# Routing logits with the gate weights as stationary operand, turned back, and the second batch's keys ahead of its block-sum values

## The chip, the cores and the metric

The kernel runs on one core of one Trainium2 chip. The metric is the device time of one launch in microseconds (us). Before the change it is 558.69 us, the median of 3 runs (557.62 to 560.31).

## The reference, cut to what matters

Three stages follow each other: local attention with block sums, a mixture of experts with one expert for each token, and a gated feed-forward layer.

```python
k_sum = k.reshape(B, H, nb, block, D).max(axis=3)
v_sum = v.reshape(B, H, nb, block, D).mean(axis=3)
...
x = attn_out.transpose(0, 2, 1, 3).reshape(B * S, H * D)     # 1536 tokens x 512
logits = x @ w_gate                                          # 8 experts
e_idx = np.argmax(logits, axis=1)
...
eom = 1.0 / (1.0 + np.exp(-(x @ w_output_gate)))
for e in range(E):
    mask = e_idx == e
    h = np.maximum(x[mask] @ w1[e], 0.0)
    out[mask] = gate_w[mask, None] * eom[mask, e, None] * (h @ w2[e])
...
gate = 1.0 / (1.0 + np.exp(-(x @ w_gate)))
return (gate * (x @ w_val)) @ w_out
```

B is 2 batches, S 768 positions, H 8 heads, D 64; a block has 32 positions and the local window 16.

## The kernel before

The order of all instructions is written out by hand; each engine works through its own queue in that order, and a semaphore wait at the head of a queue holds all that stands behind it.

**Attention** goes over 12 tiles of 128 queries (`T` from 0 to 11, six for each batch, `TB` = 6). The steps of a tile are functions. `spread_q` brings a tile's queries into the form that the score products take (on ScalarE, for two tiles on VectorE). `s1` computes masked scores in two halves, each into one PSUM bank of the ring "A" (3 banks); VectorE takes their minimum (`nm`), ScalarE the exponential (`a`). `s3` transposes `a` into the ring "B" (2 banks), and ScalarE copies it (`aT`). `s4` multiplies by the values into the one bank pair "C", and VectorE normalises (`rs`, then the tile's rows in `w2r` or `late`). `s6` transposes the result (`xT`, copied by VectorE in the first batch and by ScalarE in the second). `s7` multiplies it by `wgo`, the 16 columns of both gate weights, into a bank of "A", and VectorE copies the logits to `lg`. In loop step T the program issues `s3(T)`, `s1(T + 2)`, `s4(T)`, and `s6` and `s7` of an earlier tile.

Four parts prepare a batch: `load_k` and `ksum` (key maxima of the blocks, on VectorE, written into the key tile `kg`), `load_vr` and `vsum_part` (block sums of the values, on GpSimd or VectorE), `load_v`, and `place_sums`, which turns the sums on TensorE (line 286) and puts them into the value tiles. SyncE issues all these transfers in program order.

**Routing** of a batch is the generator `route`: one-hot choices, ranks by TensorE (lines 415 to 420), and scatters of the rows. `pick_two` and `find_first` choose the first two experts; `find_first` compares positions in six VectorE instructions (`place`, line 143). `make_table` writes the list of work items.

**Experts** are work items `i` of up to 256 tokens. `split1` and `split2` split an expert's weights into a high half (ScalarE, line 131) and a low half (VectorE, line 134); `item_T` transposes the tokens and splits them (`xTh`, `xTl`); `item_A(f)` is the first layer for 128 hidden columns, into a bank of "A" that VectorE releases with `hl` (line 655); `item_B(f)` is the second layer. Matmuls on split operands take three passes. The feed-forward layer behind it (lines 1136 and 1177) fills more than half of the time.

Of the kernel before, what the change touches and what calls it, by code (L numbers as in the profile page):

```python
# [10 lines left out]
F32 = mybir.dt.float32  # L11
# [18 lines left out]
TB = 6  # L30
NT = B * TB
# [77 lines left out]
def moe_kernel(tc, A, out):  # L109
# [153 lines left out]
    def vsum_part(b, c):  # L263

        if b not in vsum:
            vsum[b] = at.tile([128, 4, 32], F32, tag="vs", bufs=1, name=f"vs{b}")
        if b == 0 and c > 1:
            red(vsum[b][:, c, 0:NB], vrt[b, c], ALU.add)
        else:
            t, n = vrt[b, c], BLK // 2  # L270
            while n > 1:
                G.tensor_tensor(out=t[:, :, 0:n], in0=t[:, :, 0:n], in1=t[:, :, n:2 * n], op=ALU.add)
                n //= 2
            G.tensor_tensor(out=vsum[b][:, c, 0:NB], in0=t[:, :, 0], in1=t[:, :, 1], op=ALU.add)
# [100 lines left out]
    def s7(T):  # L375
        xT = st.pop(("xT", T))
        lt = bank("A", 3)
        for c in range(4):
            PE.matmul(lt[:, 0:16], xT[:, c], wgo[:, c], start=c == 0, stop=c == 3)
        V.tensor_copy(lg[:, T], lt[:, 0:16])  # L380


# [441 lines left out]
    with tc.manual_schedule():  # L824
# [19 lines left out]
            ksum(0, p)  # L844

        w2h = w2l = hh = hl = None
        q6, q8 = [], []
        order = {0: (), 1: (0,), 2: (1,), 3: (2,), 4: (3, 4)}
        ahead = {0: ((1,), ()), 1: ((2,), ()), 2: ((3,), ()), 3: ((4,), (5,))}
        spread_q(0)  # L850
# [5 lines left out]
        for T in range(NT):  # L856
            now = order.get(T, (T,))
            first, then = ahead.get(T, ((T + 2,), ()) if T < NT - 2 else ((), ()))
            q7, late7 = [t for t in q6 if t < TB or T == NT - 1], [t for t in q6 if t >= TB and T < NT - 1]
            if T < 2:  # L860
                for half in range(2):
                    s1(T + 1, (half,))
                    if T == 1 and half == 0:
                        place_sums(0)
                    s3(T, (half,))
                    if T == 0:
                        vsum_part(0, 2 + half)
                if T == 1:
                    spread_q(3)
                    spread_q(4)  # L870
            else:
                if T < NT - 1:
                    s3(T)
                if T == NT - 2:
                    s3(T + 1)
                for t in q8:
                    s7(t)
                for t in now[:-1]:
                    s4(t)
                for t in first:  # L880
                    s1(t, (0,))
                for t in q6:
                    s6(t)
                if T < NT - 3:
                    spread_q(T + 3)
                for t in first:
                    s1(t, (1,))
                if T == 7:
                    run(g, 1)
                    p1, ff = pick_two(), find_first()  # L890
                    run(p1, 1)
                    item_regs(0)
                if T == 8:
                    run(ff, 9)
                if T > 8:
                    run(g, 1)
                if T == 11:
                    item_T(0, 0, ("A", 3))
                    item_T(0, 1, ("A", 3))
            for t in now[-1:]:  # L900
                s4(t)
            for t in then:
                s1(t)
            for t in q7:
                s7(t)
            q6, q8 = list(now), late7

            if T == 0:
                load_q(4)
                for c in range(4):  # L910
                    load_vr(1, c)
            if T == 1:
                load_q(5)
                load_k(1, (0, 1))
                load_q(6)
                load_k(1, (2, 3))
                load_q(7)
                load_v(1, 0)
                load_v(1, 1)
                SP.dma_start(out=ck, in_=A["ck"])  # L920
                SP.dma_start(out=ckb, in_=A["ckb"])
                G.iota(gix, pattern=[[128, 2]], base=0, channel_multiplier=1)
                G.tensor_copy(slot, gix)
                for t0, t1 in ((0, 6), (6, 12)):
                    G.memset(xr[t0, t1][:, :, DM + 2:XW], 0.0)
                    G.iota(xr[t0, t1][:, :, DM + 1].bitcast(I32), pattern=[[128, t1 - t0]], base=128 * t0, channel_multiplier=1)
                G.memset(gidx, OOB)
                for c in range(4):
                    vsum_part(1, c)
            if T == 2:  # L930
                ksum(1, 0)
                ksum(1, 1)
            if T == 3:
                ksum(1, 2)
                ksum(1, 3)
            if 2 < T < 7:
                load_q(T + 5)
            if T == 4:
                place_sums(1)
                V.memset(low, 0.0)  # L940
                for e in range(1, 8):
                    V.memset(low[:, e, 0:e], 1.0)
            if T == 5:
                G.memset(xg[0], 0.0)
                first_st.close()
                mB_ = pool(moeA2_st, "mA2", "left")
                w1h = mB_.tile([128, 4, F], F32R, name="w1h")
                w1l = mB_.tile([128, 4, F], F32R, name="w1l")
                xTh = mB_.tile([128, 4, SLOT], F32R, name="xTh")
                xTl = mB_.tile([128, 4, SLOT], F32R, name="xTl")  # L950
                store_x(0, 3)
            if T == 6:
                store_x(3, 6)
                g = route(0)
                run(g, 2)
            if T == 7:
                run(ff, 1)
                load_w(reg["e", 0], None, range(4))
            if T > 7:
                run(g, 1)  # L960
            if T == 9:
                G.memset(xg[1], 0.0)
                split1(0)
            if T == 10:
                split1(1)
                split1(2)
            if T == 11:
                run(g, 9)
                load_w(reg["e", 0], None, range(4, 8))
                split1(3)  # L970
# [8 lines left out]
        hl = mB.tile([128, 8, SLOT], F32R, name="hl")  # L979
        run(p1, 1)  # L980
        item_A(0)
        s6(11)
        item_A(1)
        run(p1, 1)
# [2 lines left out]
        item_A(2)  # L987
        s7(11)
        item_A(3)
        run(p1, 1)  # L990
        item_regs(1)
        load_w(reg["e", 1], reg["e", 1] != reg["e", 0], range(4))
# [6 lines left out]
        item_A(6)  # L999
        split2(1)  # L1000
        item_A(7)
        run(g, 1)
        tb = make_table()
        split2(2)
        split2(3)
# [5 lines left out]
        for i in range(NSTAT):  # L1011
# [6 lines left out]
            if i:  # L1018
                for f in range(8):
                    item_A(f)  # L1020
                    if f % 2 == 0:
                        split2(f // 2)
                    elif i > 1:
                        run(bg, 1)
                    if i == 1:
                        if f in (1, 3, 4, 5):
                            run(tb, 1)
                        if f == 5:
                            item_regs(2)
                            item_gather(2, gidx[:, 2])  # L1030
            if i < NSTAT - 1:
# [2 lines left out]
            for f in range(8):  # L1034
                item_B(f, yp)
                if f % 2 == 0 and i < NSTAT - 1:
                    split1(f // 2)
                if f in (4, 5) and (f == 4 or i < NSTAT - 2):
                    item_T(i + 1, f - 4)
                if i and f in ((1, 2, 3) if i == 1 else (1, 2, 3, 6)):  # L1040
                    run(bg, 1)
                if not i and f == 0:
                    run(g, 9)
                    tail_st.close()

                    ws_st = ExitStack()
                    wsp_ = pool(ws_st, "wsp", "right")
                    yr_st = ExitStack()
                    yrp = pool(yr_st, "yrp", "right")
                    yrt = [yrp.tile([128, XW], F32, name=f"yr{k}") for k in range(4)]  # L1050
                    for t in yrt:
                        G.memset(t, 0.0)
                    cv_st = ExitStack()
                    cv = pool(cv_st, "cv", "right")

                    todo = [("w", f, k) for f in range(2) for k in range(2)]
                    bg = background(todo)
                    for k in todo[:3]:
                        load_raw(k)
                if not i and f in (1, 3, 7):  # L1060
                    run(tb, 1)
                if i == 5 and f in (0, 2, 3, 6):
                    t = (0, 2, 3, 6).index(f)
                    y_T(t)
                    load_y(t + 4, few)
                if i == 5 and f == 7:
                    split2(0)
# [180 lines left out]
```

## Time and profile before

| | |
|---|---|
| median of 3 runs | 558.69 us |
| profiled execution | 559.4 us, span 557.4 us |
| TensorE busy | 536.9 us, 96% of the span |
| VectorE busy | 385.8 us, 69% |
| ScalarE busy | 214.1 us, 38% |
| GpSimd busy | 126.7 us, 23% |
| mean granted clock of TensorE | 0.993 |

A busy TensorE means that some matmul is in flight; matmuls overlap, so the sum of durations is longer than the time they take. In the profile PE is TensorE, PEld its weight loads, DVE VectorE, ACT ScalarE, POOL GpSimd and SP SyncE. The attention stage lies before 91 us, the work items reach to about 250 us, and the feed-forward layer follows.

### The profile page before, as it was taken

To read this page: it belongs to the slowest core of one execution; us is meant where nothing else is said; L and a number is where in the kernel's file an instruction comes from. 1 tells how busy PE (TensorE), PEld (TensorE's weight loads), DVE (VectorE), ACT (ScalarE), POOL (GpSimd) and SP (SyncE) were. 2 spreads that over 40 slices of the span, in tenths; PEclk is the share of its full clock that TensorE was granted. 3 is DMA by queue.
4 is the path that set the end of the run, shared out by engine and by line. 5 is a ranking of instruction groups with operands and counts; after the bars stand their busy time and mean duration, and the time that the engine had idled before them with its cause. 6 is when DMAs were issued, how large, how long until landed. Compare 5 with 4: busy or idle time off the path is not lost.

```text
span 557.4 us, 8974 instructions
## 1 busy us (share of the span) xinstructions
PE 536.9 (96%) x3236; PEld 457.5 (82%) x3236; DVE 385.8 (69%) x735; ACT 214.1 (38%) x391; POOL 126.7 (23%) x151
## 2 busy tenths in 40 slices
PE   7799989989999999999999999999999999999995
PEld 4688979888989989867888888888888888888884
DVE  5677677789778687853687899999998763323320
ACT  3766775645546555643212112121112351212110
POOL 2673144182102100000001111111111062112211
PEclk9989999999999999998999999999999999999999
DMA  8991465972478403216123233233232000001010
GB/s 313 414 409 64 152 232 179 378 278 75 137 269 255 171 32 108 77 59 197 49 76 96 94 114 99 89 114 113 80 110 76 1 1 38 20 38 39 19 39 38
DMA packets 31983, 71.62 MB, mean 128 GB/s; under 512 B 3056, under 2 KB 11712, under 8 KB 31936
## 3 DMA queue, kind: packets, MB, share of 16 engines
q1 hardware_dynamic: 28816, 60.96, 31.5%
q0 software_dynamic: 3120, 10.06, 5.3%
q8 instruction: 26, 0.43, 0.3%
q14 instruction: 21, 0.17, 0.1%
HBM read 72.53 MB, written 11.33 MB: 150 GB/s over the span
## 4 chain that ended last, share of the span: by engine, by line
PE 34%; issue 14%; POOL 5%; ACT 0%; POOLq 0%; DVE 0%; DVEq 0%; ACTq 0%
PE ps_A L1136 18%; PE ps_B L1136 15%; POOL out_dram L1180 3%; POOL yb L134 2%; PE ps_B L746 1%; POOLq L1244 0%; ACT yb L131 0%; ACT gs L131 0%; DVE yt L141 0%; DVE gg L137 0%; POOLq L1180 0%; POOL yt L706 0%; POOLq L1084 0%; DVEq L137 0%; POOLq L134 0%
## 5 line engine op out<-in xcount | busy, mean ns | idle before, releaser
L1136 PE MATMUL ps_A<-yb,wh 128*128 128x512 f32 x312 | 97.7, 394 | 2.0 <-DVE yt L141 2.0
L1177 PE MATMUL ps_A<-yb,gs 128*128 128x512 f32 x432 | 98.1, 389 | 0.0
L1177 PEld LDWEIGHTS ps_A<-yb,gs 128*128 128x128 f32 x432 | 81.1, 188 | 16.8
L1136 PE MATMUL ps_B<-yb,wh 128*128 128x512 f32 x264 | 81.3, 389 | 0.0
L1136 PEld LDWEIGHTS ps_A<-yb,wh 128*128 128x128 f32 x312 | 58.4, 190 | 13.9 <-issue 2.4
L1136 PE MATMUL ps_A<-yb,wl 128*128 128x512 f32 x156 | 61.0, 391 | 0.0
L134 POOL TENSOR_TENSOR wl<-cvw,wh 128x512 fp32r<-128x512 f32 x20 | 26.7, 1334 | 137.9 <-ACT wh L131 137.9
L1136 PEld LDWEIGHTS ps_B<-yb,wh 128*128 128x128 f32 x264 | 49.6, 188 | 10.2
L1145 ACT ACTIVATE sg<-ps_A 128x512 f32<-128x512 f32 x36 | 21.5, 596 | 91.3 <-PE ps_A L1136 91.3
L652 PE MATMUL ps_A<-xTl,w1h 128*128 128x256 f32 x192 | 54.4, 284 | 1.5 <-DVE xTl L134 1.5
L652 PE MATMUL ps_A<-xTh,w1h 128*128 128x256 f32 x192 | 54.6, 284 | 0.0
L652 PE MATMUL ps_A<-xTh,w1l 128*128 128x256 f32 x192 | 54.3, 283 | 0.0
L1136 PE MATMUL ps_B<-yb,wl 128*128 128x512 f32 x132 | 51.3, 389 | 0.0
L131 ACT ACTIVATE gs<-gg 128x768 fp32r<-128x768 f32 x24 | 20.3, 847 | 69.5 <-PE ps_A L1177 67.4
L134 DVE TENSOR_TENSOR gs<-gg,gs 128x768 fp32r<-128x768 f32 x24 | 23.0, 958 | 34.2 <-ACT gs L131 34.1
L143 DVE TENSOR_SCALAR cva<-cva 128x512 f32<-128x512 f32 x72 | 43.3, 602 | 1.9
L134 DVE TENSOR_TENSOR w2l<-w2r,w2h 128x1024 fp32r<-128x1024 f32 x28 | 34.2, 1225 | 10.2 <-ACT w2h L131 10.0
L661 PE MATMUL yp<-w2h,hh 128*128 128x512 f32 x96 | 39.0, 406 | 0.0
L652 PEld LDWEIGHTS ps_A<-xTl,w1h 128*128 128x128 f32 x192 | 36.8, 192 | 1.9 <-DVE xTl L134 1.8
L661 PE MATMUL yp<-w2h,hl 128*128 128x512 f32 x96 | 37.5, 391 | 0.0
L661 PE MATMUL yp<-w2l,hh 128*128 128x512 f32 x96 | 37.5, 391 | 0.0
L134 DVE TENSOR_TENSOR w1l<-w1r,w1h 128x1024 fp32r<-128x1024 f32 x28 | 34.1, 1221 | 4.2 <-ACT w1h L131 4.1
(229 smaller groups left out, 967.0 us busy)
## 6 DMA issues: line engine op xcount, KB each, us to landing
w1r<-in_w_dram SPq DMA_DIRECT2D x28, 512.0 KB
w2r<-in_w_dram SPq DMA_DIRECT2D x28, 512.0 KB
raw<-in_wgv_dram SPq DMA_DIRECT2D x24, 512.0 KB
vt<-in_vv_dram SPq DMA_DIRECT2D x12, 520.0 KB
raw<-in_wo_dram SPq DMA_DIRECT2D x12, 512.0 KB
kg<-in_kg_dram SPq DMA_DIRECT2D x8, 496.0 KB
y_c<-yt SPq DMA_DIRECT2D x13, 256.5 KB
yr<-y_c SPq DMA_DIRECT2D x12, 256.5 KB
```

The source lines that it names most:

```text
L131: SC.activation(out=o, in_=i, func=AF.Copy)
L134: (eng or V).tensor_tensor(out=o, in0=i, in1=h.bitcast(F32), op=ALU.subtract)
L143: V.tensor_scalar(out=o, in0=a, scalar1=s1, scalar2=s2, op0=op0, op1=op1)
L652: PE.matmul(hp, w[:, c, s], x[:, c], start=n == 0, stop=n == 11)
L661: PE.matmul(yp[h], x[:, f, s], w[:, f], start=f == 0 and n == 0, stop=f == 7 and n == 2)
L746: PE.transpose(tp[:, c], r[:, c * 128:c * 128 + 128], ident)
L1136: PE.matmul(pp, w[:, c], x[:, c], start=n == 0, stop=n == 11)
L1145: SC.activation(out=sg, in_=pp, func=AF.Sigmoid)
L1177: PE.matmul(po, g2[:, x, f % 6], yb[f // 4][w][:, f % 4], start=f == 0 and n == 0, stop=f == 11 and n == 2)
L1180: d = G.indirect_dma_start(out=out[:, :], out_offset=bass.IndirectOffsetOnAxis(ap=row_id[:, t:t + 1].bitcast(U32), axis=0), in_=ot, in_off ...
```

## The change

`s7` now takes the gate weights as stationary operand and the tokens as moving one, so its product has 16 rows and 128 columns. VectorE copies it to a tile `lT`, and a new step `s8` transposes it back on TensorE; VectorE then copies the result to `lg` as before. Both steps take a bank of "A". `s8` of a tile stands later in the order than its `s7`: behind the next `s3` in the first batch, behind `s6` of the next tile in the second. For tile 5, `s7` stands ahead of `s4(6)`.

Besides: the keys of the second batch are loaded ahead of its block-sum values, query tiles 4 and 5 are spread later, the key maxima of the second batch are all taken in step 3, and the last of its four block sums goes to VectorE. The first split of the first expert's weights moves behind `s3` of the last two tiles. One step of the second batch's routing moves behind the first `item_B`, the token transposes of item 1 move two steps ahead, and the fills of the row buffers `yrt` move to item 1.

```diff
-        if b == 0 and c > 1:
+        if c > 1 + b:
             red(vsum[b][:, c, 0:NB], vrt[b, c], ALU.add)
...
         for c in range(4):
-            PE.matmul(lt[:, 0:16], xT[:, c], wgo[:, c], start=c == 0, stop=c == 3)
+            PE.matmul(lt[0:16, 0:128], wgo[:, c], xT[:, c], start=c == 0, stop=c == 3)
+        st["lT", T] = tl_.tile([16, 128], F32, tag="lT", bufs=2, name=f"lT{T}")
+        V.tensor_copy(st["lT", T], lt[0:16, 0:128])
+
+    def s8(T):
+        lt = bank("A", 3)
+        PE.transpose(lt[:, 0:16], st.pop(("lT", T)), ident[0:16, 0:16])
         V.tensor_copy(lg[:, T], lt[:, 0:16])
...
                 if T == 1:
                     spread_q(3)
-                    spread_q(4)
             else:
                 if T < NT - 1:
                     s3(T)
+                if T == 3:
+                    spread_q(5)
                 if T == NT - 2:
                     s3(T + 1)
+                    split1(0)
+                for t in q9:
+                    s8(t)
                 for t in q8:
                     s7(t)
...
                 for t in q6:
                     s6(t)
-                if T < NT - 3:
+                for t in q8:
+                    s8(t)
+                if 2 < T < NT - 3:
                     spread_q(T + 3)
                 for t in first:
                     s1(t, (1,))
+                if T == 2:
+                    spread_q(4)
+                if T == 3:
+                    ksum(1, 0)
+                    ksum(1, 1)
...
+            if T == TB:
+                s7(TB - 1)
             for t in now[-1:]:
                 s4(t)
             for t in then:
                 s1(t)
+            if T == TB:
+                s8(TB - 1)
+                q7 = []
             for t in q7:
                 s7(t)
-            q6, q8 = list(now), late7
+            q6, q8, q9 = list(now), late7, q7
 
             if T == 0:
                 load_q(4)
+                load_q(5)
+                load_k(1, range(4))
+            if T == 1:
+                load_q(6)
                 for c in range(4):
                     load_vr(1, c)
-            if T == 1:
-                load_q(5)
-                load_k(1, (0, 1))
-                load_q(6)
-                load_k(1, (2, 3))
                 load_q(7)
...
-                for c in range(4):
+                for c in range(3):
                     vsum_part(1, c)
-            if T == 2:
-                ksum(1, 0)
-                ksum(1, 1)
             if T == 3:
                 ksum(1, 2)
                 ksum(1, 3)
+                vsum_part(1, 3)
...
                 G.memset(xg[1], 0.0)
-                split1(0)
...
         item_A(0)
+        s8(10)
         s6(11)
...
         s7(11)
         item_A(3)
+        s8(11)
...
         item_A(7)
-        run(g, 1)
         tb = make_table()
...
                         if f == 5:
+                            for t in yrt:
+                                G.memset(t, 0.0)
                             item_regs(2)
...
-                if f in (4, 5) and (f == 4 or i < NSTAT - 2):
-                    item_T(i + 1, f - 4)
+                f0 = 4 if i else 2
+                if f in (f0, f0 + 1) and (f == f0 or i < NSTAT - 2):
+                    item_T(i + 1, f - f0)
...
-                    for t in yrt:
-                        G.memset(t, 0.0)
```

**VectorE, loop steps 2 and 3.** `nm` are the minima of scores, `ks` and `kt` the key maxima, `rs` the normalisation; names end in running numbers. Before, between the first group of key maxima and the second:

```order
L255 COPY kg_107<-ks_490 128x6x24
L146 TENSOR_REDUCE nm_517<-ps_A 128x4
L372 COPY xT_528<-ps_B 128x512
L146 TENSOR_REDUCE nm_538<-ps_A 128x4
L141 TENSOR_SCALAR rs_561<-xp_544 128x8
L360 RECIPROCAL rs_561<-rs_561 128x8
L137 TENSOR_TENSOR w2r<-xp_544,rs_561 128x512
L146 TENSOR_REDUCE nm_573<-ps_A 128x4
L146 TENSOR_REDUCE nm_584<-ps_A 128x4
L380 COPY lg<-ps_A 128x16
L146 TENSOR_REDUCE ks_596<-kg_107 128x6x2
```

After, the same stretch:

```order
L146 TENSOR_REDUCE nm_502<-ps_A 128x4
L372 COPY xT_513<-ps_B 128x512
L146 TENSOR_REDUCE nm_523<-ps_A 128x4
L146 TENSOR_REDUCE ks_529<-kg_107 128x6x2
...
L255 COPY kg_107<-ks_536 128x6x24
L141 TENSOR_SCALAR rs_560<-xp_543 128x8
L360 RECIPROCAL rs_560<-rs_560 128x8
L137 TENSOR_TENSOR w2r<-xp_543,rs_560 128x512
L146 TENSOR_REDUCE nm_572<-ps_A 128x4
L146 TENSOR_REDUCE nm_583<-ps_A 128x4
L381 COPY lT_594<-ps_A 16x128
L146 TENSOR_REDUCE ks_596<-kg_107 128x6x2
```

Both groups of key maxima now stand behind the minima of tile 4, with the normalisation of tile 2 and the minima of tile 5 between them; a copy `lT` is new.

**VectorE and TensorE, loop step 8.** `late` is the normalised tile 7, `place` the comparisons of `find_first`. VectorE before:

```order
L137 TENSOR_TENSOR late<-xp_1008,rs_1025 128x512
L143 TENSOR_SCALAR place<-ckb,o_f_983,r_pf_979 128x256 x6
L380 COPY lg<-ps_A 128x16
L146 TENSOR_REDUCE nm_1066<-ps_A 128x4
L146 TENSOR_REDUCE nm_1087<-ps_A 128x4
```

VectorE after:

```order
L137 TENSOR_TENSOR late<-xp_1028,rs_1045 128x512
L143 TENSOR_SCALAR place<-ckb,o_f_1003,r_pf_999 128x256 x6
L381 COPY lT_1078<-ps_A 16x128
L146 TENSOR_REDUCE nm_1087<-ps_A 128x4
L386 COPY lg<-ps_A 128x16
L146 TENSOR_REDUCE nm_1111<-ps_A 128x4
L146 TENSOR_REDUCE place<-ps_M 128x2
```

TensorE after, with the gate product of tile 6 (`xT`, `wgo`), the scores of tile 10 in two halves, the transposes of tile 7 (`late`) and the turn of tile 6 (`lT`):

```order
L344 MATMUL ps_B<-ident,a_857 128x128 x8
L379 MATMUL ps_A<-xT_971,wgo 16x128 x4
L312 LDWEIGHTS cmb
L312 MATMUL ps_A<-cmb 128x512
L316 MATMUL ps_A<-kg_107,qz_113 128x128 x4
L370 MATMUL ps_B<-ident,late 128x128 x4
L385 MATMUL ps_A<-ident,lT_1078 128x16
L312 LDWEIGHTS cmb
L312 MATMUL ps_A<-cmb 128x512
L316 MATMUL ps_A<-kg_107,qz_113 128x128 x4
```

The copy of tile 6's logits keeps its place behind `place`, but is now what the turn on TensorE waits for, and the second half of the scores stands behind the turn.

**VectorE and TensorE, loop steps 10 and 11.** `w1l` are low halves of weights, `late` the normalised tiles 9 and 10. VectorE before:

```order
L137 TENSOR_TENSOR late<-xp_1202,rs_1219 128x512
L134 TENSOR_TENSOR w1l<-w1r,w1h 128x4x256
L380 COPY lg<-ps_A 128x16
L141 TENSOR_SCALAR rs_1288<-xp_1271 128x8
L360 RECIPROCAL rs_1288<-rs_1288 128x8
L137 TENSOR_TENSOR late<-xp_1271,rs_1288 128x512
L134 TENSOR_TENSOR w1l<-w1r,w1h 128x4x256 x2
L380 COPY lg<-ps_A 128x16
```

VectorE after:

```order
L137 TENSOR_TENSOR late<-xp_1230,rs_1247 128x512
L134 TENSOR_TENSOR w1l<-w1r,w1h 128x4x256
L381 COPY lT_1288<-ps_A 16x128
L386 COPY lg<-ps_A 128x16
L141 TENSOR_SCALAR rs_1320<-xp_1303 128x8
L360 RECIPROCAL rs_1320<-rs_1320 128x8
L137 TENSOR_TENSOR late<-xp_1303,rs_1320 128x512
L134 TENSOR_TENSOR w1l<-w1r,w1h 128x4x256 x2
L381 COPY lT_1336<-ps_A 16x128
L386 COPY lg<-ps_A 128x16
```

TensorE after, from the score transposes of tiles 10 and 11 on:

```order
L344 MATMUL ps_B<-ident,a_1080 128x128 x8
L344 MATMUL ps_B<-ident,a_1192 128x128 x8
L379 MATMUL ps_A<-xT_1210,wgo 16x128 x4
L370 MATMUL ps_B<-ident,late 128x128 x4
L385 MATMUL ps_A<-ident,lT_1288 128x16
L354 MATMUL xp_1303<-vt_111,aT_1255 64x65 x16
L379 MATMUL ps_A<-xT_1295,wgo 16x128 x4
L370 MATMUL ps_B<-ident,late 128x128 x4
L385 MATMUL ps_A<-ident,lT_1336 128x16
L647 MATMUL ps_A<-ident,xg_87 128x128 x8
```

The copies `lT` of tiles 8 and 9 stand where the copies to `lg` stood, behind one and behind two weight splits; on TensorE the value products of tile 10 and the token transposes stand behind the two turns.

## Rows read from the trace of the kernel before

**Rows 1.** The page, part 1: busy us (share of the span) x instructions.

```profile
PE 536.9 (96%) x3236; PEld 457.5 (82%) x3236; DVE 385.8 (69%) x735; ACT 214.1 (38%) x391; POOL 126.7 (23%) x151
```

**Rows 2.** Waits of TensorE over the span: total us, times, longest us.

```profile
PE ps_B L370 <- ACT aT L345: 2.6, 2, 2.4
...
PE ps_A L1136 <- DVE yt L141: 2.0, 1, 2.0
...
PE ps_B L344 <- ACT aT L345: 1.7, 2, 1.3
...
PE ps_A L652 <- DVE xTl L134: 1.5, 1, 1.5
...
PE ps_M L415 <- DVE cum L146: 0.6, 1, 0.6
```

**Rows 3.** Timeline, 20 to 37 us: start, duration, engine; in brackets idle before.

```profile
25.61 1.28 ACT L239 ACTIVATE qz<-xg 64x512 f32<-64x512 f32 x2 [2.28 <-DMA xg<-in_q_dram]
...
28.89 1.91 PE L316 MATMUL ps_A<-kg,qz 128*128 128x128 f32 x8
...
35.41 1.05 PE L316 MATMUL ps_A<-kg,qz 128*128 128x128 f32 x8
```

**Rows 4.** Windows: busy PE, PEld, DVE, ACT, POOL, then clock, DMA share, GB/s.

```profile
29.00:30.00 1.00, 1.00 (x7) 1.00 (x6) 0.40 (x1) 0.16 (x1) 0.92 (x2) 0.50 1.03 417
...
118.00:119.00 1.00, 0.27 (x2) 0.27 (x3) 1.00 (x3) 0.52 (x1) 0.70 (x2) 1.00 1.03 419
...
253.00:254.00 1.00, 1.00 (x6) 0.90 (x5) 0.00 (x0) 0.24 (x1) 0.00 (x0) 0.50 0.07 16
```

**Rows 5.** Timeline of TensorE, 48 to 58 us.

```profile
48.74 1.06 PE L286 MATMUL sp<-ident,vs 128*24 128x128 f32 x16 [0.33 <-DVE lg L380]
...
55.08 1.96 PE L379 MATMUL ps_A<-wgo,xT 128*128 128x16 f32 x16
...
56.88 1.07 PE L344 MATMUL ps_B<-ident,a 128*128 128x128 f32 x8
```

**Rows 6.** Groups by form, TensorE, 0 to 130 us: busy us, mean ns.

```profile
L286 PE MATMUL sp<-ident,vs 128*24 128x128 f32 x32 | 2.3, 275 | 1.2 <-POOL vs L274 0.9 <-DVE lg L380 0.3
```

**Rows 7.** Timeline of VectorE, 15 to 45 us.

```profile
15.41 0.95 DVE L146 TENSOR_REDUCE vs<-w1r 128x24 f32<-128x768 f32 x1
...
41.50 0.54 DVE L146 TENSOR_REDUCE ks<-kg 128x12 f32<-128x384 f32 x1
...
44.15 0.16 DVE L141 TENSOR_SCALAR rs<-xp 128x8 f32<-128x8 f32 x1
...
45.19 0.68 DVE L146 TENSOR_REDUCE nm<-ps_A 128x4 f32<-128x512 f32 x1
```

**Rows 8.** Timeline of VectorE and TensorE, 70 to 73 us.

```profile
70.89 1.62 DVE L143 TENSOR_SCALAR place<-ckb,o_f,r_pf 128x256 bf16<-128x256 bf16 x6
...
72.43 0.17 DVE L380 COPY lg<-ps_A 128x16 f32<-128x16 f32 x1
...
71.59 0.38 PE L312 MATMUL ps_A<-cmb 67*128 67x512 bf16 x1
```

**Rows 9.** Timeline of ScalarE and TensorE, 81 to 88 us.

```profile
81.31 1.07 ACT L131 ACTIVATE w1h<-w1r 128x1024 fp32r<-128x1024 f32 x1
...
82.25 1.09 ACT L345 COPY aT<-ps_B 128x512 f32<-128x512 f32 x2
...
85.26 1.15 PE L354 MATMUL xp<-vt,aT 128*64 128x65 f32 x32
...
87.74 0.63 PE L370 MATMUL ps_B<-ident,late 128*128 128x128 f32 x4 [0.33 <-DVE late L137]
```

**Rows 10.** Timeline of VectorE, 82 to 121 us.

```profile
82.41 1.23 DVE L134 TENSOR_TENSOR w1l<-w1r,w1h 128x1024 fp32r<-128x1024 f32 x1 [0.69 <-ACT w1h L131]
...
87.51 2.35 DVE L134 TENSOR_TENSOR w1l<-w1r,w1h 128x1024 fp32r<-128x1024 f32 x2
...
120.96 0.42 DVE L655 SCALAR_TENSOR_TENSOR hl<-ps_A,hh 128x256 fp32r<-128x256 f32 x1
```

More of the change, by code (lines that the diff above doesn't have):

```diff
@@ L846, in moe_kernel @@
         w2h = w2l = hh = hl = None
-        q6, q8 = [], []
+        q6, q8, q9 = [], [], []
         order = {0: (), 1: (0,), 2: (1,), 3: (2,), 4: (3, 4)}
```

## Prediction

> **What bounds the kernel now.** I read the page first: TensorE is busy for 96% of the span [rows 1], so time can be won only where TensorE waits or where its own instructions get cheaper. The waits of TensorE are few and nearly all lie before 120 us [rows 2]: 2.4 us in one piece on the ScalarE copies of the probabilities, 1.3 us on the same kind of copy later, 1.5 us on VectorE's low half of the first expert's tokens, 0.6 us on the counts of routing, and 2.0 us in a place the change doesn't touch. Behind the 2.4 us stands a transfer: ScalarE sat 2.28 us in front of the query copy of tile 4 until its data landed, and the copies that TensorE wanted were queued behind it [rows 3]. [...] From 120 us on there is nearly no wait, so what the front gains or loses reaches the end.
>
> **Gate matmuls.** Before, a tile's logits are eight TensorE instructions that move 16 columns under 128 columns of weights; two tiles take 56.88 - 55.08 = 1.80 us, so 0.90 each [rows 5]. After, eight instructions move 128 columns under 16 columns of weights. The trace has two neighbours. Transposes of 128x128 move as many columns and go at 1.07 us for eight, about 0.11 each when pipelined [rows 5]. The block-sum transposes move 128 columns under 24 of weights: sixteen in 1.06 us, about 0.06 each [rows 5]. But one of these lasts 275 ns [rows 6], more than four starts, and they write alternately to partitions 32 and 96: two run side by side. The gate products all write partitions 0 to 15, so I take the transposes: 0.9 us, no gain; bounds 0.5 and 0.9. The turn back is two instructions more with 128 columns of weights, a quarter of the old eight: 0.22 us. Two of the twelve lie inside the next part; ten are 2.2 us.
>
> [...]
>
> **The start of the second batch's work (tiles 2 to 5).** Query copies 4 and 5 move on ScalarE behind the exponentials that TensorE needs; the 2.4 us wait goes, and with it the slow clock, at least 1.91 - 1.05 = 0.86 us. On SyncE's queue, the keys of batch 1 come ahead of its block-sum values; TensorE is then served later with values, which have until the block-sum transposes at 48.74 [rows 5]; I cost that at nothing, with GpSimd's idle time as cover (one of four sums moves to VectorE). TensorE would be 3.3 us ahead. What is late next is VectorE: the key maxima of batch 1, two groups of about 44.15 - 41.50 = 2.65 us [rows 7], now both lie after the minima of tile 4, and behind them a block sum of 0.95 [rows 7]. Ahead of tile 3's normalisation stand: a minimum 0.7 [rows 7], a group 2.65, a normalisation 1.1 (from 86.4 to 87.51 [rows 9, 10]), two minima 1.3, a group 2.65, the sum 0.95, two small copies 0.35: 9.7 us. From the end of tile 4's scores, 36.46 before and about 33.2 after [rows 3], that gives 42.9 for tile 3's normalisation in place of 44.15 [rows 7]: 1.25 of the 3.3. The durations overlap by some tenths, and a 0.33 us wait at 48.74 goes too [rows 5]. I take -2.0, bounds -3.3 and -1.2.
>
> **The copies of the turned logits.** Each turn back waits for a copy on VectorE, and VectorE works in order. Before, the copy of the logits held nobody on TensorE; now the next scores, value products or expert matmuls are queued behind the turn. At three places a long piece stands ahead of the copy.
> (a) Tile 6: six placements, 1.62 us, end only at 72.43, where the logits copy starts (0.17) [rows 8]. TensorE wants to go on at 71.59 [rows 8]. With the handing over, 72.74 - 71.59 = +1.15. A small wait of TensorE on ScalarE just behind it is swallowed (0.2, what the longest of the two on those copies leaves [rows 2]): +0.95.
> (b) Tile 8: the first weight split has moved behind the copies of both last tiles. That takes away the 1.3 us wait, of which about 0.3 stays: -1.0. But VectorE's half of the split stands ahead of tile 8's copy. From the end of the last score transposes: a ScalarE copy 0.55 (two take 1.09), the high half 1.07, the low half 1.23, the logits copy 0.2 [rows 9, 10]: 3.05. TensorE comes after gate products 0.9 and transposes 0.45: 1.35. Wait +1.7.
> (c) Tile 9: two splits, 2.35 us, end at 89.86; with copy and handing over 90.17 [rows 10]. TensorE has finished its transposes at about 87.74 + 0.45 = 88.2 [rows 9]. Wait +1.95, in the order as it stands, since both count from the value products at 85.26.
>
> **The first expert.** The rank matmuls go behind six matmuls of the second layer: the 0.6 us wait is covered by their 1.4 us; -0.6. The token transposes of item 1 move two steps ahead; VectorE's low halves then come ahead of two weight splits: -1.5. What is late next is the same VectorE queue: without gaps up to the first hidden half at 120.96 [rows 10], and nothing is taken from it. The fourth hidden tile needs the PSUM bank which that half releases. All of that queue starts later by what the front lost, so the wait passes to this bank nearly whole: +1.4, bounds 0 (it fits) and 1.5 (the whole of the old wait). The fills of the row buffers move to an idle stretch of GpSimd; nothing.
>
> **Sum.** +2.2 - 2.0 + 0.95 - 1.0 + 1.7 + 1.95 - 0.6 - 1.5 + 1.4 = +3.1 us. It is made on the profiled execution, which took 559.4 (span 557.4), 0.7 above the median of 558.69; I put it on the median: 561.8.
>
> **Rivals.**
> 1. The clock falls in (c). A wait of 2.0 us was followed by 0.50, one of 1.5 not [rows 4]; (c) is 1.95, with 1.7 shortly before. Price 0.86 for one group of scores and as much again for its neighbours, about 1.6: 563.4. Against it: the predicted wait is on the edge.
> 2. The gate products do run at the pace of the block-sum transposes, 0.5 us. It counts in the six tiles where TensorE isn't held by VectorE: 6 x 0.4 = 2.4: 559.4. For it: a row with few weight columns exists; against it: that row has two column groups.
> [...]
> 3. Faster: the copies don't hold TensorE, because VectorE is through with the splits and placements when TensorE comes. (a), (b), (c) lose 0.95 + 1.7 + 1.95 = 4.6; the sum is -1.5, and if the bank wait is also absent -2.9: 557.2 to 555.8. It decides where each copy is done within about 1.3 us of the transposes before it. The order of VectorE's queue speaks against it.
> 4. The change doesn't win the second batch's start, because VectorE's key maxima take all of it or because the query data land later: -2.0 becomes 0: 563.8.
>
> **How the numbers follow.** Forecast 0.50 (560.3 to 563), rival 1 0.15, rival 2 0.15, rival 3 0.12, rival 4 0.08. A measurement here can tell about 0.5%, 2.8 us, from no change: the bounds are 555.9 and 561.5. Slower: half of the forecast and a little more, 0.27, with rivals 1 and 4: 0.50. Faster: most of rival 3 with what is left over of rival 2 when both meet: 0.12. Same: 0.38. The range leaves out about 1 in 10 on each side: 557.2, the upper end of rival 3, to 563.6, between rivals 1 and 4.
>
> **What would show it.** In the trace after, TensorE's long waits should be on the copy of the turned logits, three of them, 1.2 to 2 us, around 71, 85 and 90 us; no wait of 2 us on ScalarE at 25 us and a clock of 1.00 from 24 to 36; the gate products at about 0.11 us from start to start. The first expert's first matmul should start about 3 us later than before, and no wait on the low token half near 117. Wrong I am if the gate products go at 0.06, if the copies come early, or if the expert starts earlier than before.

## The result and the profile after

The changed kernel took 563.69 us (median of 11 runs, 562.38 to 565.78); the kernel before took 559.38 us beside it (11 runs). The ratio is 1.0085, with a 95% interval of 1.0067 to 1.0103: about 4.75 us more. The forecast was 3.1 us more, 561.8. The profiled execution of the changed kernel took 563.34 us, with a span of 561.4 us.

The page's part 1 and the waits of TensorE over the span (total us, times, longest us):

```profile
PE 541.0 (96%) x3248; PEld 456.6 (81%) x3248; DVE 389.8 (69%) x748; ACT 213.7 (38%) x391; POOL 124.2 (22%) x146
```

```profile
PE ps_A L385 <- DVE lT L381: 4.9, 4, 1.7
...
PE ps_A L1156 <- DVE yt L141: 2.2, 1, 2.2
PE ps_A L658 <- DVE hl L661: 1.0, 2, 0.7
...
PE ps_B L370 <- ACT aT L345: 0.6, 1, 0.6
```

TensorE is busy for 4.1 us more [rows 1]. The 2.4 us wait on the copied probabilities and the 1.5 us wait on the low token half are gone, and the 1.3 us one has shrunk to 0.4 [rows 2]. In their place stands one new line of 4.9 us: the turn back (L385) waits for the copy of the turned logits, lT. TensorE's timeline has the three long waits and a shorter one, and VectorE's has what stands ahead of each of the long ones:

```profile
38.81 0.23 PE L385 MATMUL ps_A<-ident,lT 16*128 16x16 f32 x1 [0.62 <-DVE lT L381]
...
46.58 1.06 PE L286 MATMUL sp<-ident,vs 128*24 128x128 f32 x16 [0.68 <-DVE w2r L137]
...
63.93 0.66 PE L370 MATMUL ps_B<-ident,late 128*128 128x128 f32 x4 [0.60 <-ACT aT L345]
...
67.91 1.05 PE L379 MATMUL ps_A<-xT,wgo 128*16 128x128 f32 x8
68.89 0.39 PE L312 MATMUL ps_A<-cmb 67*128 67x512 bf16 x1
...
72.09 0.23 PE L385 MATMUL ps_A<-ident,lT 16*128 16x16 f32 x1 [1.00 <-DVE lT L381]
72.25 0.39 PE L312 MATMUL ps_A<-cmb 67*128 67x512 bf16 x1
...
82.42 1.14 PE L344 MATMUL ps_B<-ident,a 128*128 128x128 f32 x8 [0.40 <-ACT aT L345]
...
86.65 0.23 PE L385 MATMUL ps_A<-ident,lT 16*128 16x16 f32 x1 [1.52 <-DVE lT L381]
...
91.65 0.23 PE L385 MATMUL ps_A<-ident,lT 16*128 16x16 f32 x1 [1.74 <-DVE lT L381]
91.81 1.09 PE L647 MATMUL ps_A<-ident,xg 128*128 128x128 f32 x8
92.83 1.91 PE L354 MATMUL xp<-vt,aT 128*64 128x65 f32 x32
```

```profile
70.22 1.62 DVE L143 TENSOR_SCALAR place<-ckb,o_f,r_pf 128x256 bf16<-128x256 bf16 x6
71.76 0.27 DVE L381 COPY lT<-ps_A 16x128 f32<-16x128 f32 x1
...
85.18 1.23 DVE L134 TENSOR_TENSOR w1l<-w1r,w1h 128x1024 fp32r<-128x1024 f32 x1 [3.00 <-ACT w1h L131]
86.32 0.27 DVE L381 COPY lT<-ps_A 16x128 f32<-16x128 f32 x1
...
89.06 2.35 DVE L134 TENSOR_TENSOR w1l<-w1r,w1h 128x1024 fp32r<-128x1024 f32 x2
91.33 0.27 DVE L381 COPY lT<-ps_A 16x128 f32<-16x128 f32 x1
```

What to see: at 72, 87 and 92 us TensorE waits 1.00, 1.52 and 1.74 us, and each time the 16x128 copy of 0.27 us comes right behind six placements or one or two halves of a weight split. The copy is short; its place in VectorE's queue is what costs. The fourth wait, 0.62 us at 38.81, was not forecast; it is 1.54, 1.15 and 1.60 us in experiments 2, 3 and 8. No run shows what it costs by itself: experiment 9, with the old gate products, waits 0.71, 0.58 and 0.84 us in the same stretch for other things. Eight gate products take 68.89 - 67.91 = 0.98 us from their start to the next instruction, and a turn back 72.25 - 72.09 = 0.16. Behind the third wait the 32 value products last 1.91 us instead of the usual 1.15 [rows 9]; the window there shows why (busy PE, PEld, DVE, ACT, POOL, then clock, DMA share, GB/s):

```profile
94.00:95.00 1.00, 1.00 (x16) 0.81 (x15) 0.60 (x3) 0.54 (x1) 0.00 (x0) 0.50 0.92 324
```

The granted clock is 0.50. From 92 to 97 us the five windows show 0.99, 0.50, 0.50, 0.50 and 0.80, which loses 0.01 + 3 x 0.50 + 0.20 = 1.7 us. The block-sum transposes start at 46.58 instead of 48.74 [rows 5], the first expert's first matmul at 96.47 instead of 91.17: 5.3 us later, 1.7 of them the slow clock of this one execution, where about 3 were forecast. The new wait of 0.60 us at 63.93 is one that the prediction didn't have.

### The profile page after: what moved, and what is told of

Read it like the earlier page. It is cut to its first block, busy times and chain, and to the rows that moved or that the text cites. A ratio compares the mean times of both kernels' runs of the same rounds, so it can differ in the third digit from the quotient of the medians.

```text
span 561.4 us, 9007 instructions
## 1 busy us (share of the span) xinstructions
PE 541.0 (96%) x3248; PEld 456.6 (81%) x3248; DVE 389.8 (69%) x748; ACT 213.7 (38%) x391; POOL 124.2 (22%) x146
## 4 chain that ended last, share of the span: by engine, by line
PE 34%; issue 14%; POOL 5%; ACT 0%; POOLq 0%; DVE 0%; DVEq 0%; ACTq 0%
PE ps_A L1156 18%; PE ps_B L1156 15%; POOL out_dram L1200 3%; POOL yb L134 1%; PE ps_B L752 1%; POOLq L1264 0%; ACT yb L131 0%; ACT gs L131 0%; DVE yt L141 0%; DVE gg L137 0%; POOLq L1200 0%; POOL yt L712 0%; POOLq L1104 0%; DVEq L137 0%; POOLq L134 0%
## 5 line engine op out<-in xcount | busy, mean ns | idle before, releaser
L658 PEld LDWEIGHTS ps_A<-xTh,w1h 128*128 128x128 f32 x192 | 36.8, 191 | 2.2 <-DVE hl L661 1.4
```

Of the source, the lines that this page charges most:

```text
L658: PE.matmul(hp, w[:, c, s], x[:, c], start=n == 0, stop=n == 11)
```

## The experiments

Each was timed in five rounds beside the kernel before. The last two columns are worked out: the mean of the granted clocks that the timed runs list, and the time against before at one common clock. For that, a straight line was laid through the 199 runs of these kernels and of before on three chips, with a level for each kernel and each chip and one slope; the slope is 0.36 us per 0.001 of mean clock.

| kernel | us, median | ratio to before, 95% | mean clock | us against before at one clock |
|---|---|---|---|---|
| before (83 runs) | 558.58 to 559.95 | 1 | 0.9932 | 0 |
| changed | 563.69 | 1.0085 (1.0067 to 1.0103) | 0.9954 | not in the line: no second kernel on its chip |
| 1 old gate products | 556.79 | 0.9965 (0.9948 to 0.9982) | 0.9957 | -1.70 |
| 2 wait filled | 563.74 | 1.0089 (1.0062 to 1.0116) | 0.9953 | +5.17 |
| 3 turns later | 561.55 | 1.0044 (1.0019 to 1.0069) | 0.9960 | +3.30 |
| 4 front undone | 563.25 | 1.0110 (1.0073 to 1.0146) | 0.9955 | +5.92 |
| 5 front alone | 558.38 | 0.9976 (0.9952 to 1.0000) | 0.9948 | -0.90 |
| 6 first expert alone | 560.43 | 1.0007 (0.9985 to 1.0028) | 0.9921 | -0.35 |
| 7 split alone | 559.52 | 0.9983 (0.9960 to 1.0006) | 0.9928 | -0.90 |
| 8 turns later, other bank | 560.58 | 1.0008 (0.9986 to 1.0030) | 0.9950 | +0.95 |
| 9 all but the logits | 555.56 | 0.9947 (0.9926 to 0.9969) | 0.9947 | -2.50 |
| 10 front and split | 556.11 | 0.9954 (0.9936 to 0.9973) | 0.9962 | -1.54 |
| 11 front, split, rank | 556.24 | 0.9959 (0.9942 to 0.9976) | 0.9960 | -1.59 |

**1. Old gate products, the rest of the change kept.** In the changed kernel:

```
-            PE.matmul(lt[0:16, 0:128], wgo[:, c], xT[:, c], ...)
-        st["lT", T] = tl_.tile([16, 128], F32, ...)
-        V.tensor_copy(st["lT", T], lt[0:16, 0:128])
+            PE.matmul(lt[:, 0:16], xT[:, c], wgo[:, c], ...)
+        V.tensor_copy(lg[:, T], lt[:, 0:16])
     def s8(T):
+        pass
```

> The changed kernel with the gate products of before (128 columns of weights, 16 columns moved, logits copied at once) and no turn back; all other edits of the change stay. Theory: the turned logits cost 4.3 us in three waits on the copy (1.00, 1.52, 1.74), 1.7 us in the slower clock behind the third, 10 x 0.16 = 1.6 us in turns and 10 x 0.05 = 0.5 us in dearer gate products, together 8.1; some wait on the probabilities comes back at the end. Time 555.6 us, 554.5 to 557.5, which is below before. Rival: the other edits win nothing that lasts (the start of the second batch and the first expert give back what they gain), then the time is that of before, 558.5 to 560.

Measured: 556.79 us, below before and about 6.7 us below the changed kernel (1.0085 - 0.9965 = 0.0120). The rival falls: the other edits win, and the logits lose more than they win. The 8.1 us of the theory held the 1.7 us of the slow clock; without it the sum is 6.4. Tile 5's gate products still stood ahead of its value products in this kernel, with the same late wait:

```profile
64.05 0.66 PE L370 MATMUL ps_B<-ident,late 128*128 128x128 f32 x4 [0.55 <-ACT aT L345]
...
65.65 0.17 PE L418 MATMUL ps_M<-cum,ckb 128*128 128x16 bf16 x1
```

**2. The third wait filled with useless work.** Ahead of tile 9's turn back: `for k in range(12): PE.transpose(w[:, 0:128], ident, ident)`, into a bank that nobody reads.

> The changed kernel with twelve extra 128x128 transposes, some 1.4 us of useless TensorE work whose result nobody reads, put into the 1.74 us wait ahead of tile 9's turn back. Theory: the clock fell behind this wait because TensorE stood idle; filled, the granted clock stays at 1.00 between 92 and 97 us and the kernel with more work is faster by 1.7 us: 562.0, 561.2 to 562.8. Rival: the clock falls there for another reason, or the fall costs nothing: 563.7, 563.2 to 565.

Measured: 563.74 us, no gain; the ratio is 1.0089, against 1.0085 for the changed kernel. In its trace the wait shrinks to 0.43 us, the transposes cost nothing and the clock stays at 1.00:

```profile
90.85 1.47 PE L897 MATMUL ps_M<-ident 128*128 128x128 f32 x12
92.75 0.23 PE L385 MATMUL ps_A<-ident,lT 16*128 16x16 f32 x1 [0.43 <-DVE lT L381]
```

But the fourth experiment keeps the whole wait of 1.74 us, and its clock doesn't fall either (timeline, and the window that answers to the one above):

```profile
92.88 0.23 PE L385 MATMUL ps_A<-ident,lT 16*128 16x16 f32 x1 [1.74 <-DVE lT L381]
...
94.06 1.16 PE L354 MATMUL xp<-vt,aT 128*64 128x65 f32 x32
```

```profile
94.00:95.00 1.00, 1.00 (x34) 0.94 (x32) 0.64 (x2) 1.00 (x3) 0.00 (x0) 1.00 0.80 137
```

So the fall behind this wait belongs to the profiled execution of the changed kernel and not to each run. That idleness causes it isn't refuted by this. That filling the wait pays 1.7 us (0.0030) in the median is just outside the noise: the ratio rose by 0.0004, give or take 0.0032.

**3 and 8. Each turn back one step later; then also another bank.** Experiment 3 moves `s8(t)` of tiles 6 to 10 behind the gate products of the next tile, tile 9's and 10's behind hidden tiles of the first expert. Experiment 8 adds:

```
-                    item_T(0, 1, ("A", 3))
+                    item_T(0, 1)
```

> The changed kernel with each turn back of tiles 6 to 10 issued one step later on TensorE, behind the gate products of the next tile (tile 9's behind the first hidden tile of the first expert); nothing is left out. Theory: VectorE has made the copies by then, the three waits (4.3 us) and the slow clock (1.7 us) go: 557.7 us, 556.7 to 559. Rival: the waits only pass on, to the token transposes or the first expert's matmuls, whose weight and token halves come from the same VectorE queue: 561.5 to 563.5.

> The kernel with the turns back one step later, and beside it the second token transposes of the first item write the other pair of PSUM banks. Theory: in the kernel with the turns later these transposes waited 1.30 us for the bank that tile 9's copy on VectorE frees; with a bank that this copy doesn't hold the wait goes: 560.3 us, 559.6 to 561. Rival: the same VectorE queue holds the next user of a bank or the first expert's token halves: 561.2 to 562.

Experiment 3 won 1.0085 - 1.0044 = 0.0041, 2.3 us; its 561.55 us lie at the lower end of the rival's range. The first two waits are gone; the third passed on, not through the turn but through its PSUM bank. The second token transposes take the bank which tile 9's copy has yet to read:

```profile
88.90 0.60 PE L647 MATMUL ps_A<-ident,xg 128*128 128x128 f32 x4
90.80 0.66 PE L647 MATMUL ps_A<-ident,xg 128*128 128x128 f32 x4 [1.30 <-DVE lT L381]
```

With the other pair of banks (experiment 8) nothing waits there, and the 560.58 us lie in the theory's range:

```profile
88.50 0.60 PE L647 MATMUL ps_A<-ident,xg 128*128 128x128 f32 x4
88.94 0.60 PE L647 MATMUL ps_B<-ident,xg 128*128 128x128 f32 x4
```

From the changed kernel to this one the ratio falls by 1.0085 - 1.0008 = 0.0077, 4.3 us (1.6 to either side is noise); the three waits together are 1.00 + 1.52 + 1.74 = 4.26. In the traces less of it lasts. From the block sums to the wait on the output rows it is 256.95 - 47.70 = 209.25 us in experiment 2, whose third wait is filled but lasts as long, and 253.20 - 47.23 = 205.97 here: 3.3 us less, with a new wait of 0.51 us on the way. So the close match of 4.3 and 4.26 is partly luck.

```profile
47.70 1.06 PE L286 MATMUL sp<-ident,vs 128*24 128x128 f32 x16 [0.68 <-DVE w2r L137]
...
256.95 0.73 PE L1160 MATMUL ps_A<-yb,wh 128*128 128x512 f32 x2 [2.15 <-DVE yt L141]
```

```profile
47.23 1.06 PE L286 MATMUL sp<-ident,vs 128*24 128x128 f32 x16 [0.68 <-DVE w2r L137]
...
77.28 0.38 PE L312 MATMUL ps_A<-cmb 67*128 67x512 bf16 x1 [0.51 <-DVE lg L386]
...
253.20 0.73 PE L1157 MATMUL ps_A<-yb,wh 128*128 128x512 f32 x2 [2.21 <-DVE yt L141]
```

The kernel is level with the one before: the turned logits have eaten all that the other edits win, even without the three waits.

**4 and 5. The front undone, the front alone.** The loads, query copies, key maxima and block sums at the start of the second batch go back to their old places in the changed kernel (4), or to the new ones in the kernel before (5), as in the diff.

> The changed kernel with the start of the second batch's work (query, key and value loads, query copies 4 and 5, key maxima, block sums) as before. Theory: this part won 2.2 us at the block-sum transposes, and its loss reaches the end: 565.9 us, 565 to 567, with the 2.4 us wait and the clock of 0.50 near 28 us back. Rival: its gain is taken back by the later waits on VectorE, which stay where they are: 563 to 564.2.

> The kernel before with only the start of the second batch's work changed (queries, keys and values loaded in the new order, query copies 4 and 5 later, key maxima 0 and 1 of the second batch after tile 4's scores, one block sum on VectorE). Theory: from the value products at 21 us to the block-sum transposes it saves 1.6 us (26.2 to 25.3 us in three kernels that have it against 27.1 to 27.5 in two that don't), and this reaches the end: 557.1 us against 558.7, 556.3 to 557.8. Rival: what it saves is spent before the end, at the copies of the probabilities around 64 and 83 us, where ScalarE is no earlier than before: 558.2 to 559.2.

Undone, the median of 563.25 us lies in the rival's range, but two of the six runs took 566.20 and 567.55 us, at a mean clock of 0.992 and 0.989, and the ratio rose by 1.0110 - 1.0085 = 0.0025, 1.4 us, no more than noise (0.75 us against experiment 2 at one clock). Alone, the front wins 0.0024, 1.3 us, with an interval from 0 to 2.7. All of these are less than the 2.2 us which the profile seemed to show, though the noise doesn't exclude it. What the front saves hangs on the clock: the long wait on the probabilities stood in four of the profiles, and only in two of these did the clock fall behind it, to 0.50. In experiment 4 it was 2.43 us long, the clock stayed at 1.00, and from the first value products at 20.74 us to the block sums it took 27.1 us; before, with the fall, 48.74 - 21.26 = 27.5; with the front alone 47.19 - 22.11 = 25.1. The other one of the four without a fall, experiment 6, has 46.87 - 21.01 = 25.9, so that there the front would have saved 0.8 by this kernel, and next to nothing by experiments 1, 9, 10 and 11, which have the front and the old gate products and take 25.5 to 25.8.

**7. The first split alone.** `split1(0)` behind tile 11's copies instead of at the end of tile 9's step.

> The kernel before with only the first weight split moved behind the copies of the last tiles' probabilities. Theory: the 1.3 us wait shrinks to 0.4 and 0.4 comes back at the next transposes: -0.5, 558.2 us, 557.4 to 558.9. Rival: the split's low half comes so late that the next normalisation, or the first expert, waits for all of it: 559 to 560.

0.0017, 0.95 us, with an interval that holds nothing to 2.2. Its trace has what was expected: 0.39 us in place of 1.3 at the copies, and 0.74 at the next transposes. Further on the rank matmuls wait 2.18 us instead of 0.62.

```profile
82.30 1.15 PE L344 MATMUL ps_B<-ident,a 128*128 128x128 f32 x8 [0.39 <-ACT aT L345]
...
87.55 0.63 PE L370 MATMUL ps_B<-ident,late 128*128 128x128 f32 x4 [0.74 <-DVE late L137]
```

**6, 10 and 11. The first expert's edits alone; front and split; these and the rank matmuls.** The edit of 11 against 10 is one line, a `run(g, 1)` less behind the first expert's last hidden tile.

> The kernel before with only the first expert's edits (rank matmuls behind six matmuls of the second layer, token transposes of item 1 two steps ahead, the fills of the row buffers later). Theory: the waits of 0.6 and 1.5 us go and 1.0 us on the PSUM banks of hidden tiles come: -1.1, 557.6 us, 556.8 to 558.2. Rival: the banks take all that is won, since VectorE's queue sets the pace there: 558.3 to 559.2.

> The kernel before with the front and the first weight split alone. If the parts add up: 0.9976 x 0.9983 = 0.9959 (0.994 to 0.998). Against the kernel that has the first expert's edits too it says what these are worth: theory, nothing, since the 2.1 us of waits that they take away come back at the PSUM banks (2.6 us on the low hidden halves in the profile of these edits alone); rival, they win about 1.1 us when the front is early, and this kernel is slower than that one by 0.002.

> The kernel with the front and the split, and beside them only the rank matmuls behind six matmuls of the second layer. Theory: the wait on the counts, 0.6 us before, 1.2 with the front alone and 2.2 with the split alone, is the one edit of the first expert that lasts: 0.6 to 1.5 us below the kernel without it, ratio 0.994 to 0.995. Rival: the low hidden halves hold the PSUM banks anyhow: no difference.

Alone the edits give no gain that can be measured. Experiment 10 shows that front and split add up: 0.9954 measured, 0.9959 expected. With 11 the rival holds, but by another wait: the rank matmuls' 0.62 us is passed whole to the low token half, which waited 1.45 us in experiment 10 and 2.16 in 11:

```profile
102.86 0.17 PE L415 MATMUL ps_M<-cum,ckb 128*128 128x16 bf16 x1 [0.62 <-DVE cum L146]
...
116.71 0.39 PE L652 MATMUL ps_A<-xTl,w1h 128*128 128x256 f32 x1 [1.45 <-DVE xTl L134]
```

```profile
115.94 0.39 PE L652 MATMUL ps_A<-xTl,w1h 128*128 128x256 f32 x1 [2.16 <-DVE xTl L134]
```

The edit of the rank matmuls alone pays nothing. That it pays together with the token transposes is argued from experiment 9; the token transposes were not moved by themselves. With both and the front early (experiment 9) the first expert loses 1.0 us on the banks, and alone (experiment 6) 2.6:

```profile
PE ps_A L652 <- DVE hl L655: 2.6, 3, 1.2
```

From the first expert's first matmul to the third item's it is 50.1 us in experiment 9 and 50.9 in 10: 0.8 us. In the median the difference is 0.55 us and no more than noise.

**9. Everything but the logits.** The kernel before with front, split and first expert's edits; against experiment 1 tile 5's gate products stand where they stood before.

> The kernel before with the front, the first weight split and the first expert's edits, and nothing of the logits part; against the kernel with the old gate products it differs only in tile 5, whose gate products stand behind its successors' scores again, as before, and not ahead of the value products. Theory: the other place of tile 5's gate products delays tile 5's successors by 0.6 to 0.8 us (a 0.55 us wait on the probabilities at 64 us, 18.2 us from the block sums to the rank products in place of 17.45), so this kernel is below the one with the old gate products: ratio to before 0.995 (0.9935 to 0.9965). Rival: that delay is swallowed by the wait on the splits at 82 us or by the first expert, and the ratio stays at 0.9965.

555.56 us, the fastest of all and below both kernels. Against experiment 1 it is 0.0018, 1.0 us, lower, in the theory's range, but the intervals overlap. In the traces the difference is plain: from the block sums to the rank products 64.02 - 46.56 = 17.46 us here, as before, and 65.65 - 47.44 = 18.21 in experiment 1, with no wait on the probabilities here:

```profile
46.56 1.06 PE L286 MATMUL sp<-ident,vs 128*24 128x128 f32 x16 [0.66 <-DVE lg L380]
64.02 0.17 PE L415 MATMUL ps_M<-cum,ckb 128*128 128x16 bf16 x1
...
248.15 0.73 PE L1139 MATMUL ps_A<-yb,wh 128*128 128x512 f32 x2 [1.99 <-DVE yt L141]
```

The difference lasts: at the wait on the output rows it is 248.15 - 46.56 = 201.59 us here and 249.84 - 47.44 = 202.40 in experiment 1, 0.8 more.

```profile
47.44 1.06 PE L286 MATMUL sp<-ident,vs 128*24 128x128 f32 x16 [0.66 <-DVE lg L380]
...
249.84 0.92 PE L1153 MATMUL ps_A<-yb,wh 128*128 128x512 f32 x2 [1.99 <-DVE yt L141]
```

## Why the prediction was too low

Its direction and its places were right; its sum, +3.1, was 1.6 us short of what was measured (the interval of the ratio is +3.7 to +5.8). None of its own signs of being wrong came. The median that it was put on, 558.69 from three runs, lay another 0.7 below the 559.38 measured beside the changed kernel.

- **Gate matmuls.** Taken at 0.9 for eight, no gain; measured 0.92 (two tiles in 54.89 - 53.04 = 1.85) to 0.98. The old ones were not always 0.90: some of the second batch take 0.81 (83.89 to 84.70). The pace of the f32 transposes (eight in 63.45 - 62.54 = 0.91 us before) was the right neighbour and rival 2 falls. The turns back were taken at 0.22 and took 0.16. Tile by tile the dearer gate products add up to about 0.8, so that ten tiles cost 10 x 0.16 + 0.8 = 2.4 instead of 2.2.
- **Copies of the turned logits.** (a) 1.00 against a predicted wait of 1.15, (b) 1.52 against 1.7, (c) 1.74 against 1.95. The sum was 4.6 in the forecast and 4.26 in the trace; taking all three away gave back 4.3 in the time, with 1.6 of noise to either side, and 3.3 in the trace. Rival 3 falls.
- **Tile 5's gate products: the step that failed.** The working costed the gate matmuls and the turn back, and never where tile 5's stand. They go ahead of its value products, so that routing of the first batch has its logits in time. This shifts what follows: a wait of 0.55 to 0.61 us on the probabilities at 64 us stands in all six profiles with this move and in none of the seven without it, and the price is 18.21 - 17.46 = 0.75 us at the rank products and 0.8 at the output rows; by the times 1.0, not settled alone. The whole logits part costs 209.25 - 201.59 = 7.7 us from the block sums to the output rows (experiment 2 against 9); by the times 1.0085 - 0.9947 = 0.0138, 7.7 us as well (6.1 to 9.3). The forecast had 6.8, and tile 5 is what it lacks. That the rest comes out even to a tenth is partly luck, since its terms are off by 0.2 to 0.4.
- **The other edits: a mis-sized term.** Front, split and first expert were to win 2.0 + 1.0 + 0.7 = 3.7; together they win 0.0053, 3.0 us (1.7 to 4.1, which holds 3.7 too). Split and first expert win 203.13 - 201.59 = 1.5 us of the forecast 1.7 in the traces, from the block sums at 48.74 to the output rows at 251.87 before and in experiment 9. That leaves the front as the second part of the miss: alone it wins 1.3 instead of 2.0, though 2.0 lies within its noise. The 2.0 was read off one execution, in which the clock fell to 0.50 behind the 2.4 us wait [rows 4] and eight score products took 1.91 us there against 1.05 later [rows 3]; it fell in two of four profiles.
- **The clock (rival 1).** It did fall in (c) in the profiled execution, at the price named, 1.7 for 1.6. But it was argued as a threshold between waits of 1.5 and 2.0 us, and that is wrong. The same 1.74 us wait went without a fall in experiment 4, at a clock of 1.00 from 90 to 98 us. The medians of the changed kernel don't hold this price: its runs have a mean clock of 0.9954, above the 0.9932 that before has on other chips.
- **Rival 4** (the front wins nothing) named the median to 0.1 us, 563.8, but by luck: alone, the front wins 1.3 us in the median, and half of the miss is tile 5's place.

By the traces tile 5's place is 0.8 of the missing 1.6 us and the split and first expert 0.2. The rest is put down to the front by subtraction, and this stays open: no run settles the front's worth to better than a microsecond.

## What to carry to other kernels

Turning a product so that the small operand is stationary saved nothing here: eight f32 matmuls took 0.81 to 0.92 us with 16 columns moved under 128 of weights, and 0.92 to 0.98 the other way round. And it makes a copy, which nobody waited for, a link between two TensorE instructions: read what stands ahead of that copy in its engine's queue, and issue the second instruction late, with a look at who takes its PSUM bank. A wait that is removed must be followed to the next one on the same queue: the rank matmuls' 0.62 us came back in full 13 us later. And a profile is one execution: a fall of the clock in it is a draw, not a term of the sum, unless several executions show it.

## What was not expected of the hardware

The fall of the clock behind a wait is no function of the wait's length here. In thirteen profiles the wait on the output rows near 252 us lasted 2.0 to 2.2 us in every one; the granted clock fell behind it in eight (to 0.50 in three windows of 1 us in the kernel before; to a mean of 0.57 to 0.74 over the lowest window of 4 us in each of the eight) and not in five, the changed kernel with its 2.2 us among these. The wait of 2.2 to 2.4 us near 27 us was followed by a fall to 0.50 in two of four, and one of 2.18 us at 106 us in experiment 7 by another, to a mean of 0.62 and 0.53 over 106 to 108 and 108 to 110 us. A wait of 1.34 us in experiment 5 was followed by one, to 0.50 from 84 to 86 us:

```profile
81.33 1.15 PE L344 MATMUL ps_B<-ident,a 128*128 128x128 f32 x8 [1.34 <-ACT aT L345]
84.00 2.00 PE L354 MATMUL xp<-vt,aT 128*64 128x65 f32 x32
```

The same wait of 1.34 us in the kernel before was not: the clock was 1.00 from 80 to 90 us [rows 9: its value products at 85.26 took 1.15]. A fall lost 1.7 us of full clock each time, added up over the windows of 1, 2 or 4 us. Over the changed kernel's eleven runs the mean clock goes with about two thirds of the scatter (squared correlation 0.65; 0.03 to 0.99 for the other kernels): its three runs with a mean clock of 0.998 or 0.999 took 562.38 to 562.69 us, its two with 0.992 took 564.82 and 565.78. So the mean clock varies from run to run of the same kernel, here from 0.992 to 0.999.
